# Block-sparse attention and a maxout feed-forward on one core: one PE visit per unit for scores and for values, single PSUM banks, queries of 256

## The chip, the core and the metric

The kernel runs on one core of one Trainium2 chip. Five engines work side by side there: PE (matrix products, which read on-chip memory and write PSUM, eight banks of 128 x 512 fp32), DVE (vector work), ACT (activation functions, copies), POOL (vector work that cannot reach PSUM, and gathers) and SP (which issues most DMAs here). The metric is the time of one launch in device microseconds, as a median of runs. Lower is better.

## What is computed

For 4 batches and 8 heads, with 768 positions of width 64, attention runs over blocks of 32 positions. A query block sees its own block and its two neighbours, the first and the last block, and three blocks drawn for it; the first and the last query block see everything. A maxout feed-forward follows.

```python
scores = scale * np.matmul(q, k.transpose(0, 1, 3, 2))
mask = np.abs(blk_i - blk_j) <= window
mask = mask | (blk_i == 0) | (blk_j == 0) | (blk_i == n_blocks - 1) | (blk_j == n_blocks - 1)
...
scores = np.where(mask, scores, -1000000000.0)
attn = np.exp(scores - np.max(scores, axis=-1, keepdims=True))
attn = attn / (np.sum(attn, axis=-1, keepdims=True) + 1e-09)
...
h = np.maximum(np.maximum(x @ w1, x @ w2), x @ w3)     # x: 3072 x 512, h: 3072 x 768
return (h @ w_out).astype(np.float32)
```

The four weight matrices come as 64-bit floats (3.1 MB each), the rest as fp32.

## The kernel before, in words

**Precision.** Every product is made of three fp16 passes: each operand is split into a high part and a low remainder (`PASSES`: high x high, high x low, low x high). Before the split a tensor is scaled by a power of two that comes from its sum of squares (`scale_of`, L317).

**Units.** A batch has 12 units. Eleven are *sparse*: two neighbouring query blocks with all eight heads. One (`"G"`) is *global*: the first and the last block, which see all 768 keys. Before, the global unit comes first in a batch. Four units make a *tile* of 256 rows of `x`, so there are 12 tiles.

**A sparse unit** is worked in two items of four heads. `gather` (L586) copies a query block's key blocks into `kg` (DVE, POOL and ACT each one of the drawn blocks, DVE the window) and fetches the value rows from a copy in DRAM (`vscr`) by an indirect DMA on POOL's queue. `sparse_item` (L663) then has: 24 matmuls of scores into a pair of banks (L677); on DVE the row maximum (L656) and from it the bias of the exponential (L658); two exponentials on ACT (L686); `probs` (L619), which splits the probabilities into high (ACT, L635) and low (POOL, L636) and turns them with a DMA transpose (L639), or, in the first four units, turns them on PE (L628); and 48 matmuls of values into `av_ps` (L701). `finish_unit` (L752) divides by the sums, turns the result on PE (L768) and splits it into `xg`. A global unit has four items of one head pair member each, with 12 matmuls of 384 columns of scores (L720) and 36 of values (L742).

**The feed-forward** (`feed_forward`, L779) of a tile makes 18 groups of 12 matmuls (L795, moving operand 256 wide), of which three at a time are reduced by a maximum (ACT L799, DVE L802), splits the result (ACT L805, POOL L806), and makes 2 x 3 groups of 6 matmuls of 512 columns (L819); ACT scales them (L825) and SP stores them.

**PSUM.** Two pairs of banks for scores (`s_pss`), one bank for values, two for the feed-forward in turn, one for everything that is turned or summed (`tp_one`); early on, one score pair may serve for turning too.

**Preparation.** K is loaded, squared for its sum (ACT, L462), turned on PE (L492) and split; V likewise without turning, and written to `vscr` (L524). Q comes in 24 tiles of 128 queries (L534 on), each with its square pass (L543), its scale (L319 to L324, L550, L551), a turn (L559) and a split. The weights are decoded from 64-bit patterns by hand (`decode_w`, L348): 24 loads land in four buffers (parts of `kt` and `xg`), POOL casts one part (L371), DVE joins it (L375) into a buffer in `ht`, ACT squares it (L386), and ACT and DVE split it (L398, L406).

**What sets the order.** Nothing is ordered at run time: every step is entered with `plan.add(engine, cost, ...)`, and `Plan.order` (L76) simulates the engines with these costs, always taking the ready step with the smallest `pri`. On PE it prefers feed-forward after feed-forward unless an attention step has waited over 3 us or more than two wait. The result is one fixed list of instructions for each engine; on the chip each engine runs its list in that order and waits on semaphores.

## Time and profile before

| what | us |
|---|---|
| median of 3 runs | 695.38 (691.42 to 697.71) |
| span of the profiled execution | 687.5 |
| median above that span | 7.9 |
| PE busy | 591.3 |
| DVE busy | 411.8 |
| ACT busy | 392.1 |
| POOL busy | 316.8 |

The profile gives the profiled execution's span, from its first to its last instruction, and no wall time of that same execution; the third row of the table is the distance of the median run to it. In the forty slices of the page the granted PE clock is between 0.5 and 0.6 in most of the first tenth to quarter, and 0.9 or more after it:

```profile
PE   2586468359999979999999789989999789999997
PEclk9756559559999989999999999999999999999999
```

Each digit is a slice of 17.2 us, in tenths. A line such as `L795 PE MATMUL f_ps<-xg,w_hl 128*128 128x256 f16 x2592 | 308.4, 278 | ...` names the source line, the engine, the operation, what it writes and reads, shape and count, then busy time, the mean duration in ns, and the idle time ahead of it. Matmuls overlap, so their mean duration (278 ns) is not what one of them costs; the distance between starts is.

### The profile page before, as it was taken

To read this page: it belongs to the slowest core of one execution; us is meant where nothing else is said; L and a number is where in the kernel's file an instruction comes from. 1 tells how busy PE (TensorE), PEld (TensorE's weight loads), DVE (VectorE), ACT (ScalarE), POOL (GpSimd) and SP (SyncE) were. 2 spreads that over 40 slices of the span, in tenths; PEclk is the share of its full clock that TensorE was granted. 3 is DMA by queue.
4 is the path that set the end of the run, shared out by engine and by line. 5 is a ranking of instruction groups with operands and counts; after the bars stand their busy time and mean duration, and the time that the engine had idled before them with its cause. 6 is when DMAs were issued, how large, how long until landed. Compare 5 with 4: busy or idle time off the path is not lost.

```text
span 687.5 us, 25107 instructions
## 1 busy us (share of the span) xinstructions
PE 591.3 (86%) x10576; PEld 442.2 (64%) x10576; DVE 411.8 (60%) x1022; ACT 392.1 (57%) x830; POOL 316.8 (46%) x414
## 2 busy tenths in 40 slices
PE   2586468359999979999999789989999789999997
PEld 2354347236885856875876666866776675778684
DVE  1678779983666876498555664676547675422110
ACT  4646667667636766776547656855558556312121
POOL 1354356463534665364554563446455756511110
PEclk9756559559999989999999999999999999999999
DMA  9684788779967799987997889996987979830000
GB/s 212 187 249 131 233 217 202 159 151 221 222 121 169 92 200 211 199 198 165 169 169 138 148 177 174 195 234 132 188 126 148 176 144 174 175 61 25 17 17 32
DMA packets 197044, 109.28 MB, mean 159 GB/s; under 512 B 161073, under 2 KB 182594, under 8 KB 196930
## 3 DMA queue, kind: packets, MB, share of 16 engines
q1 hardware_dynamic: 187074, 72.51, 57.1%
q0 software_dynamic: 9856, 35.15, 20.5%
q8 instruction: 83, 1.36, 0.9%
q14 instruction: 31, 0.25, 0.1%
HBM read 68.72 MB, written 12.70 MB: 118 GB/s over the span
## 4 chain that ended last, share of the span: by engine, by line
PE 70%; DVE 13%; issue 9%; ACT 2%; DMA 2%; POOL 1%; SPq 1%; DVEq 0%; POOLq 0%; ACTq 0%
PE f_ps L795 37%; PE f_ps L819 13%; PE av_ps L701 5%; PE s_ps L677 4%; PE s_ps L720 2%; DVE nm L656 2%; PE tp_ps L559 2%; PE tp_ps L492 1%; DVE nm L658 1%; PE tp_ps L768 1%; PE tp_ps L332 1%; DVE w_hl L406 1%; DVE vhl L520 1%; DVE kg L602 1%; PE av_ps L742 1%
## 5 line engine op out<-in xcount | busy, mean ns | idle before, releaser
L795 PE MATMUL f_ps<-xg,w_hl 128*128 128x256 f16 x2592 | 308.4, 278 | 15.7 <-issue 7.3
L795 PEld LDWEIGHTS <-w_hl 128*128 128x128 f16 x2592 | 254.6, 100 | 58.4 <-issue 23.5
L636 POOL TENSOR_TENSOR phl<-pr,phl 128x512 f16<-128x512 f32 (+1 forms) x106 | 119.1, 1130 | 81.1 <-ACT phl L635 51.8
L802 DVE SCALAR_TENSOR_TENSOR hf<-f_ps,hf 128x256 f32<-128x256 f32 x144 | 60.7, 421 | 114.6 <-PE f_ps L795 103.3
L806 POOL TENSOR_TENSOR ht<-hf,ht 128x256 f16<-128x256 f32 x72 | 50.4, 701 | 147.2 <-ACT ht L805 147.0
L686 ACT ACTIVATE pr<-s_ps,nm,qsm 128x256 f32<-128x256 f32 x176 | 92.2, 564 | 40.7 <-DVE nm L658 27.9
L608 POOL DMA_INDIRECT vg<-vscr,rows_of x88 | 83.6, 950 | 53.4 <-PE av_ps L701 37.2
L819 PE MATMUL f_ps<-wo_hl,ht 128*128 128x512 f16 x432 | 98.7, 380 | 0.0
L656 DVE TENSOR_REDUCE nm<-s_ps 128x2 f32<-128x512 f32 x88 | 60.2, 684 | 24.9 <-PE s_ps L677 18.5
L805 ACT CAST ht<-hf 128x256 f16<-128x256 f32 x72 | 28.9, 403 | 79.0 <-DVE hf L802 78.9
L819 PEld LDWEIGHTS <-ht 128*128 128x128 f16 x432 | 40.8, 98 | 46.9 <-issue 3.1
L635 ACT CAST phl<-pr 128x512 f16<-128x512 f32 (+1 forms) x106 | 61.7, 592 | 5.7 <-DMA pts<-phl 5.3
L595 POOL COPY kg<-kt 128x256 f16 x88 | 37.9, 450 | 53.8 <-PE s_ps L677 41.1
L701 PE MATMUL av_ps<-vg,pts 128*32 128x65 f16 (+1 forms) x4224 | 50.3, 200 | 13.2 <-issue 7.4
L701 PEld LDWEIGHTS <-pts 128*32 128x32 f16 x4224 | 41.5, 98 | 29.0 <-issue 20.9
L677 PE MATMUL s_ps<-kg,qt 64*32 64x256 f16 x2112 | 48.5, 294 | 10.8 <-ACT pr L686 4.4
L658 DVE TENSOR_SCALAR nm<-nm,qsm 128x2 f32<-128x2 f32 (+1 forms) x104 | 46.5, 448 | 2.2
L799 ACT ACTIVATE hf<-f_ps 128x256 f32<-128x256 f32 x72 | 27.5, 382 | 30.8 <-PE f_ps L795 30.3
L595 ACT COPY kg<-kt 128x256 f16 x88 | 32.7, 404 | 16.7 <-PE s_ps L677 13.2
L677 PEld LDWEIGHTS <-qt 64*32 64x32 f16 x2112 | 24.3, 95 | 22.7 <-issue 13.3
L825 ACT ACTIVATE ob<-f_ps,vsm 128x512 f32<-128x512 f32 x24 | 16.5, 686 | 26.9 <-PE f_ps L819 26.8
L595 DVE COPY kg<-kt 128x256 f16 x88 | 30.6, 381 | 1.5 <-issue 1.3
(138 smaller groups left out, 661.2 us busy)
## 6 DMA issues: line engine op xcount, KB each, us to landing
kt<-in_moe_w_dram SPq DMA_DIRECT2D x14, 511.0 KB, 4.1
vscr<-vhl SPq DMA_DIRECT2D x12, 520.0 KB, 4.5
stage<-in_k_dram SPq DMA_DIRECT2D x24, 256.0 KB, 5.6
stage<-in_v_dram SPq DMA_DIRECT2D x12, 512.0 KB, 8.0
qn<-in_q_dram SPq DMA_DIRECT2D x20, 256.0 KB, 5.0
out_dram<-ob SPq DMA_DIRECT2D x20, 256.0 KB, 2.1
vg<-vscr SPq DMA_DIRECT2D x16, 130.0 KB, 3.8
kt<-in_moe_w_out_dram SPq DMA_DIRECT2D x4, 511.8 KB, 4.6
```

Of the source, the lines that this page charges most:

```text
L595: (A.copy if t == 2 else eng.tensor_copy)(out=dst, in_=src)
L608: plan.add("POOL", 1.02, lambda c=c: L.indirect_dma_start(out=vgj[: 6 * HB, c].rearrange("p e h x -> p (e h x)"), out_offset=None, in_=vsc ...
L635: plan.add("ACT", 0.05 + 0.565 * n / 512, lambda: A.copy(out=hl[:, :n], in_=prt[:, :n]), r=[("pr", it % NPR)], w=[hk], pri=pri)
L636: plan.add("POOL", 1.2 * n / 512, lambda: L.tensor_tensor(out=hl[:, n : 2 * n], in0=prt[:, :n], in1=hl[:, :n], op=ALU.subtract), r=[("pr", ...
L656: plan.add("DVE", 0.7, lambda: V.tensor_reduce(out=n[:, 0:2], in_=both()[:, :, :256], axis=AX.X, op=ALU.max), w=[ks], pri=pri, drop=job)
L658: plan.add("DVE", 0.23, lambda: V.tensor_scalar(out=n[:, 2 : 2 + w], in0=n[:, :w], scalar1=sm[:, 5:6], scalar2=LN_TOP, op0=ALU.mult, op1=A ...
L677: T.matmul(out=s_ps[r * BS : (r + 1) * BS, hd * 512 : hd * 512 + 256], lhsT=q_t[hp, tq, 2 * i + u, q0 + c * BS : q0 + (c + 1) * BS], rhs=k ...
L686: plan.add("ACT", 0.56, lambda hd=hd: A.activation(out=prt[:, hd * 256 : hd * 256 + 256], in_=s_of(job)[:, hd * 512 : hd * 512 + 256], fun ...
L701: T.matmul(out=av_ps[r * BS : (r + 1) * BS, 2 * i + hd, :w], lhsT=pv[:, tp, hd, e, r * BS : (r + 1) * BS], rhs=vgj[:, c, e, h, (D + 2) * t ...
L795: T.matmul(out=pf, lhsT=w_hl[f][:, j, g, wp], rhs=x[:, g, xp, :], start=g == 0 and n == 0, stop=g == G - 1 and n == 2)
L802: plan.add("DVE", 0.42, lambda h=h, pf=pf: V.scalar_tensor_tensor(out=h, in0=pf, scalar=2.0 ** -14, in1=h, op0=ALU.mult, op1=ALU.max), r=[ ...
L819: T.matmul(out=f2_ps, lhsT=hts[:, f, hp, t * P : (t + 1) * P], rhs=wo_hl[f // 3][:, f % 3, wp], start=f == 0 and n == 0, stop=f == NF - 1 ...
```

## The change

Nearly every function is touched. What it does:

1. **One visit for a unit.** `sparse_item` becomes `sparse_unit`: all 48 matmuls of a unit's scores are one step, head pair members in two single banks, and all 96 of its values one step. Probabilities are still made in two halves. The global unit has four score steps of 12 matmuls with both members of a head pair in one group, and two value steps of 72.
2. **Banks singly.** All eight banks are `psb[0..7]`; a step takes one (or two single ones) of any that is free, up to a limit by kind: scores 4, values 2, turns and sums 2, feed-forward 3, early turns 6.
3. **Queries of 256.** 12 Q tiles of 256 queries in place of 24 of 128; the rows of a tile are laid out in even and odd positions, so `xg` is read with runs of 32 elements.
4. **Sparse units first** in batch 0; in later batches the global unit leads its tile. The first 8 units (4 before) turn their probabilities on PE.
5. **Squares on PE** for batch 0's K, V and first Q tile and for all weights: the upper 16 bits of the fp32 words, read as bf16, are multiplied with themselves in 128 x 128 blocks, and DVE sums the diagonal. Later batches keep ACT's square passes.
6. **Weights decoded in place**, and into twelve landing places; POOL or ACT may cast.
7. The bias of the exponential goes from DVE to ACT, with one operation for a unit. The table of gathered rows is made on DVE from one load of the sampled blocks. The first K and Q are loaded with longer runs and turned by plain fp32 matmuls with the identity.
8. **The planner** gets new costs, a model of the clock, of a port that DVE and POOL share and of DMA, and ranks each step by the due time of the feed-forward group that needs it, with written-out offsets for each kind of step (`OFFS`).

The core of the diff:

```diff
-    s_pss = [ps.tile([P, 1024], F32, name=f"s_ps{i}") for i in range(2)]
-    av_ps = ps.tile([P, 4, 65], F32, name="av_ps")
-    f_ps = [ps.tile([P, DM], F32, name=f"f_ps{i}") for i in range(2)]
-    tp_one = ps.tile([P, 512], F32, name="tp_ps")
+    psb = [ps.tile([P, 512], F32, name=f"ps{i}") for i in range(8)]
...
+    LIMIT = dict(s=4, a=2, t=2, f=3, k=6)
...
+    def squares_on_pe(parts, pri):
...
+                hi = top(view)
+                for y in range(0, n, P):
+                    T.matmul(out=bank(j)[:, :P], lhsT=hi[:, y : y + P], rhs=hi[:, y : y + P],
+                             start=x == 0 and y == 0, stop=x == len(parts) - 1 and y == n - P)
...
+        plan.add("DVE", 0.25, lambda: V.scalar_tensor_tensor(
+            out=junk[:, :P], in0=bank(j)[:, :P], scalar=1.0, in1=ident, op0=ALU.mult, op1=ALU.mult, accum_out=ssq[c]),
...
-            plan.add("DVE", 0.69, lambda st=st, k=k, y=y: V.scalar_tensor_tensor(
-                out=mi[:, k], in0=st.bitcast(I32).rearrange("p (x w) -> p x w", w=2)[:, :, 0], scalar=13, in1=y,
+            plan.add("DVE", 0.6, lambda st=st, y=y: V.scalar_tensor_tensor(
+                out=st.bitcast(I32)[:, :512], in0=st.bitcast(I32).rearrange("p (x w) -> p x w", w=2)[:, :, 0], scalar=13, in1=y,
...
+            for hd in range(2):
+                c0 = ((2 * g + hd) * 2 + e) * D
+                T.matmul(out=tv(y)[hd * D : hd * D + D], lhsT=st[:, c0 : c0 + D], rhs=ident, start=True, stop=True)
...
-        plan.add("DVE", 0.23, lambda: V.tensor_scalar(
-            out=n[:, 2 : 2 + w], in0=n[:, :w], scalar1=sm[:, 5:6], scalar2=LN_TOP, op0=ALU.mult, op1=ALU.add),
+        plan.add("ACT", 0.2, lambda: A.activation(
+            out=nb[:, 4:8], in_=nb[:, 0:4], func=AF.Identity, bias=ln_top, scale=sm[:, 5:6]),
...
+            for i in range(2):
+                for n, (tq, tk) in enumerate(PASSES):
+                    for r in range(4):
+                        u, c = r // 2, r % 2
+                        for hd in range(2):
+                            hp = slice(hd * 64, hd * 64 + 64)
+                            T.matmul(
+                                out=bank(j, hd)[r * BS : (r + 1) * BS, i * 256 : i * 256 + 256],
...
+        plan.add("PE", 0.70, scores, r=QK(F) + KG(jg), w=["s_turn"], pri=pri, mode="s", take=j, lat=0.95, cold=0.7)
...
+        plan.add("PE", 0.78, values, r=keys + VG(jg), w=["a_turn", ("unit", U)], pri=pri, mode="a", take=av, lat=1.0, cold=0.4)
...
-                            T.matmul(out=pf, lhsT=w_hl[f][:, j, g, wp], rhs=x[:, g, xp, :],
+                            T.matmul(out=bank(fj)[:, :256], lhsT=w_hl[f][:, j, g, wp], rhs=x[:, :, xp, :, g].rearrange("p n e x -> p e n x"),
...
-    order = ["G", NU - 1] + list(range(NU - 1))
+        for n in (2, 0, 1) if b else (0, 2, 1):
+            ms = [4 * n + x for x in range(4)]
+            ms = [m if m < 11 else "G" for m in ms]
+            if n == 2 and b:
+                ms = ["G"] + ms[:3]
```

More of the change, by code (lines that the diff above doesn't have):

```diff
@@ L134, in order @@
+            for job, k in op.drop:
+                job["left"][k] -= 1
+                job["end"][k] = max(job["end"][k], done + self.HOP)
+                if not job["left"][k]:
+                    banks[job["banks"][k]] = slots[job["kind"]][job["slots"][k]] = job["end"][k]
             for s in succ[i]:
[L135 to L136 removed]
+                ready[s] = max(ready[s], done + self.HOP)
@@ L137, in order @@
                 left[s] -= 1
                 if not left[s]:
-                    cands[ops[s].eng].add(s)
-        self.times = out
-        return [ops[i].emit for _, i in sorted(out)]
+                    for e in ops[s].forms:
+                        cands[e].add(s)
+        self.times, self.by = out, by
+        self.end = max(free.values())
+        return [ops[i].forms[by[i]][3] for _, i in sorted(out)]
 @with_exitstack
@@ new lines, in registers @@
+    def registers(t, name, first, pri):
+        blocks = slice(first, min(first + TB, NB - 1))
+        n = blocks.stop - blocks.start
+        def load():
+            _, values = nc.values_load_multi_w_load_instructions(
+                samp[0:1, blocks, t, 0], engines=[(ET.DVE, ET.Pool, ET.Activation)[t]], min_val=0, max_val=NB - 1)
+            for x, value in enumerate(values):
+                regs[t, first + x] = value
+        plan.add(name, 0.35 + 0.25 * n, load, r=["samp"], w=[("regs", t, first + x) for x in range(n)], pri=pri)
@@ L883, in tile_block_sparse_attention_maxout_ffn @@
+    plan.rank(KN["start"], KN["tile"], KN["stretch"])
+    emits = plan.order(KN["hold"], KN["att"], KN["queue"])
     with tc.manual_schedule():
```

1106 lines of the change are left out of this document (618 added, 488 removed).

## The prediction, made before the changed kernel ran

> **What bounds the kernel now.** I read the page first (busy times, the forty slices, the chain), then the windows view cut where the work changes, then PE's groups and waits in the longest stretch.
>
> ```profile
> span 687.5 us, 25107 instructions
> PE 591.3 (86%) x10576; PEld 442.2 (64%) x10576; DVE 411.8 (60%) x1022; ACT 392.1 (57%) x830; POOL 316.8 (46%) x414
> PE 70%; DVE 13%; issue 9%; ACT 2%; DMA 2%; POOL 1%; SPq 1%; DVEq 0%; POOLq 0%; ACTq 0%
> ```
> ```profile
> 0.00:97.00 97.00, 53.20 (x822) 36.41 (x823) 65.77 (x158) 58.94 (x111) 39.48 (x74) 0.67 0.73 201
> 97.00:174.00 77.00, 56.65 (x1045) 40.42 (x1047) 56.12 (x134) 52.82 (x108) 39.48 (x45) 0.75 0.88 189
> 174.00:620.00 446.00, 417.86 (x8219) 315.93 (x8214) 279.01 (x705) 267.41 (x584) 229.81 (x284) 0.98 0.89 166
> 620.00:687.50 67.50, 63.55 (x508) 49.47 (x506) 10.93 (x27) 12.90 (x29) 8.02 (x12) 1.00 0.06 21
> ```
> In the window rows the columns after the length are the busy time of PE, its weight loads, DVE, ACT and POOL, then the granted clock, the DMA share and GB/s. Four stages show. Until 97 us no feed-forward matmul can run: PE is busy 53.2 of 97 at a clock of 0.67 and DVE, at 65.8, is the busiest. From 97 to 174 only the first of the twelve feed-forward tiles is done, with PE idle for 77.0 - 56.65 = 20.35 us. From 174 to 620 PE is busy 417.9 of 446 (94%) at clock 0.98: it is the bound there, and 28.1 us is idle. At the end two tiles run alone:
>
> ```profile
> 620.85 23.58 PE f_ps L795 x216
> 644.43 7.77 PE f_ps L819 x36
> 652.20 23.58 PE f_ps L795 x216
> 675.78 7.78 PE f_ps L819 x36
> ```
> A tile is thus 23.58 + 7.77 = 31.35 us of matmuls at full clock (109 and 216 ns each), twelve are 376 us. The change leaves these matmuls as they are, so 376 us is the part that no schedule shortens; what can go is the time before and around them.
>
> The profiled execution's span is 687.5; the runs' median of 695.38 lies 7.9 us above it (the fastest run 3.9). I work with the span and add 7.9 at the end. A measurement of this kernel can tell about 1% from no change.
>
> **Stage 1, until the first feed-forward matmul (97 us).** Removed from the path: the six small loads of sampled blocks and POOL's long row of small operations for the row table (now one load and DVE work), the ACT square passes of batch 0 and of the weights (now 128x128 bf16 products on PE and a diagonal sum on DVE), the global unit as first unit (sparse units come first), and the reuse of four landing buffers for weights. Added: K and Q of the first tile are turned by plain fp32 matmuls, and units 4 to 7 also have their probabilities turned on PE. PE is idle for 97 - 53.2 = 43.8 us here, which covers the added PE work; without that cover it would cost its own time: 8 turns of 8 matmuls, from 8 times the 1.09 us of the old turn (9 us, bound 0 net) to 64 times the longest row for a cold fp32 matmul here, 0.415 us (27 us, so 18 more).
>
> ```profile
> 14.19 1.09 PE L492 MATMUL s_ps<-ident,stage 128*128 128x128 f32 x4
> ```
> ```profile
> L492 PE MATMUL s_ps<-ident,stage 128*128 128x128 f32 x16 | 4.0, 415 | 3.6 <-DVE qt L564 2.8 <-DVE vsm L319 0.8
> ```
> The Trainium skill (Perfetto Trace Analysis, Transposes) says to use the transpose and not a standard matmul for a transpose, which speaks against these turns. The row above shows only the transpose; if the page's loss were all exposed, the sum would be up to 18 us higher.
>
> The start is then set by DVE, whose list hardly shrinks. It has no data for about 10 us; 65.8 us of work at 98% occupancy gives 10 + 67 = 77 us. So I take -20 us, with bounds 0 (DVE just as loose as now) and -27 (four units at 70 us).
>
> **Stage 2, the first tile beside the weights (77 us).** Before, its second product could start only when the last weights were split:
>
> ```profile
> L375 DVE SCALAR_TENSOR_TENSOR ht<-xg,ob x6: 680/683/746, 51.2 to 140.7; 128x512 int32<-128x512 int32 x6
> L398 ACT ACTIVATE wo_hl<-ht,w_t x6: 707/710/721, 147.0 to 151.4; 128x512 f16<-128x512 f32 x6
> L819 PE MATMUL f_ps<-wo_hl,ht x432: 376/380/391, 164.4 to 683.2; 128*128 128x512 f16 x144
> ```
> The columns after the name are min/median/max in ns and the first and last start. Decoding ran from buffer to buffer until 141 us, over these loads and ten like them:
>
> ```profile
> kt<-in_moe_w_dram SPq DMA_DIRECT2D x14, 511.0 KB, 4.1
> ```
> With the decoded form written into the landing place, all 24 loads (12.3 MB) have a place early; at the 201 GB/s of stage 1 they alone need 61 us, so they can have landed by 80 to 100 us beside K, Q and V. PE's 20.35 us of idle goes, and most of the half-rate excess of this tile:
>
> ```profile
> L795 PE MATMUL f_ps<-xg,w_hl 128*128 128x256 f16 x216 | 29.5, 303 | 4.6 <-ACT hf L799 4.6
> ```
> 29.5 against 23.58 is 5.9 us. Together -26.3 at most, 0 at least; I take -24, since the first few us will still be at half clock. Four more turned units put 56 + 24 = 80 instead of 48 transposes of probabilities on PE: 32 more at 0.2 us (between 0.27 us for two warm ones, the two starts below, and 0.41 us for a cold one) is +6 us, bounds +4 and +13.
>
> ```profile
> L628 PE MATMUL tp_ps<-ident,pr 128*128 128x128 f32 x17 | 4.6, 411 | 2.5 <-ACT pr L730 2.1 <-DVE pts L631 0.4
> 326.18 0.44 PE L768 MATMUL tp_ps<-ident,xr 128*128 128x128 f32 x2
> 326.45 4.09 PE L795 MATMUL f_ps<-xg,w_hl 128*128 128x256 f16 x36
> ```
>
> **Stage 3, PE-bound (446 us).** One visit in place of two is cheap to price from neighbours: the start of the next visit minus the start of this one.
>
> ```profile
> 309.29 0.56 PE L701 MATMUL av_ps<-vg,pts 128*32 128x65 f16 x48
> 309.77 0.52 PE L677 MATMUL s_ps<-kg,qt 64*32 64x256 f16 x24
> 310.23 0.56 PE L701 MATMUL av_ps<-vg,pts 128*32 128x65 f16 x48
> ```
> ```profile
> 304.17 0.98 PE L701 MATMUL av_ps<-vg,pts 128*32 128x65 f16 x96
> 305.09 0.33 PE L492 MATMUL tp_ps<-ident,stage 128*128 128x128 f32 x1
> ```
> ```profile
> 382.12 0.85 PE L677 MATMUL s_ps<-kg,qt 64*32 64x256 f16 x48
> 382.89 0.59 PE L701 MATMUL av_ps<-vg,pts 128*32 128x65 f16 x52
> ```
> Half a unit's values take 0.48, a whole one 0.92; half a unit's scores 0.46, a whole one 0.77. So a unit gains at most 0.04 + 0.15 us, and if all of the 1584/48 = 33 sparse units here came in halves, 6 us; 22 units' scores and some values do, so -4 (0 to -6). The headline of the change is worth little by itself.
>
> The global scores gain more: they now run both heads of a pair in one group, four tiles of the array at a time, where 12 matmuls used two:
>
> ```profile
> 209.19 1.16 PE L720 MATMUL s_ps<-kt,qt 64*64 64x384 f16 x12
> 210.29 0.44 PE L768 MATMUL tp_ps<-ident,xr 128*128 128x128 f32 x2
> ```
> 1.10 us each, and 144/12 = 12 of them here; at half, -6.6 (bounds 0 and -6.6; that head pairs do run together the sparse scores show, 24 matmuls of 256 columns in 0.46 us). The sums of squares have a bf16 instead of an fp32 product and half as many Q tiles: the three groups below (10.5 us) come down to about 16 visits of some 0.3 us, -5 (-3 to -8).
>
> ```profile
> L332 PE MATMUL tp_ps<-qsm,ones 128*128 128x1 f32 x36 | 6.6, 252 | 0.7 <-DVE xg L773 0.7
> L332 PE MATMUL tp_ps<-vsm,ones 128*128 128x1 f32 x18 | 2.4, 247 | 0.0
> L332 PE MATMUL tp_ps<-ksm,ones 128*128 128x1 f32 x12 | 1.5, 237 | 0.0
> ```
> The 28.1 us of idle is what freer banks should cut: any job may take any of eight banks, feed-forward groups have three instead of two, scores four single ones, and the values their own two.
>
> ```profile
> L795 PE MATMUL f_ps<-xg,w_hl 128*128 128x256 f16 x1944 | 231.4, 277 | 11.0 <-issue 7.3 <-DVE hf L802 3.7
> L701 PE MATMUL av_ps<-vg,pts 128*32 128x65 f16 (+1 forms) x3504 | 38.9, 195 | 7.6 <-issue 7.4 <-DVE xr L761 0.2
> L658 DVE TENSOR_SCALAR nm<-nm,qsm x104: 203/228/3021, 32.5 to 592.2; 128x2 f32<-128x2 f32 x88, 128x1 f32<-128x1 f32 x16
> ACT pr L686 <- DVE nm L658: 27.9, 22, 5.6
> ```
> The bias of the exponential also leaves DVE, where an operation of 228 ns sometimes lasted 3.0 us and ACT waited 27.9 us for it, for one ACT operation per unit. I take -18 of the 28 (0 to -25). Strided reading of the feed-forward's moving operand (runs of 32 elements) I cost at nothing: the sparse scores already read runs of 16 at full rate. Off PE: DVE loses the 104 bias operations and half of the Q scalings; ACT, POOL and SP stay below two thirds busy.
>
> **Stage 4.** The two lone tiles are not shortened by the change; PE does the same work sooner or later.
>
> **The sum.** -20 - 24 + 6 - 4 - 6.6 - 5 - 18 = -71.6; 687.5 - 71.6 = 615.9; + 7.9 = **624 us**. All best bounds together (-27 - 26 + 4 - 6 - 6.6 - 8 - 25 = -95) give 601, all worst (+18 + 13 - 3) 723.
>
> **Rivals.**
> *Start not shortened* (0.13): DVE, not the landing places, paces the weights: 24 decodes and 24 splits stay on it. For: it is the busiest engine of both first stages. Against: decode waited for its inputs and buffers. Then stage 1 stays and stage 2 gives 10 of its 24: 624 + 20 + 14 = 658 us. The Trainium skill (SBUF — State Buffer, Who interferes with whom) says that a DVE operation with two SBUF inputs and a GpSimd operation reading SBUF exclude each other for their whole length; the decode and POOL's cast remain such a pair, and the 3.0 us operation above agrees, so I keep this rival above a tenth.
>
> *DMA is the bound of stage 3* (0.11):
>
> ```profile
> q1 hardware_dynamic: 133024, 44.68, 62.7%
> q0 software_dynamic: 7840, 27.96, 25.3%
> DMA to landing us min/median/max: 2.8/5.9/10.4
> ```
> In stage 3 the queues' packets fill 62.7 + 25.3% of sixteen engines, and transposes and gathers per unit stay the same. If 0.89 is all there is, stage 3 keeps its length and only stages 1 and 2 gain: 624 + 4 + 6.6 + 5 + 18 = 658 us. Against: PE's waits there name no DMA.
>
> *Values hold the queue* (0.05, the slower side): PE's order is fixed, and a unit's values now start only when both its transposes have landed (2.8 to 10.4 us). Each us of lateness stalls PE with the feed-forward behind it. From 78 us over the forecast it is slower by 1%: 44 sparse units by 1.8 us each, giving 702 us. Against: 7.6 us of idle before the values in all of stage 3.
>
> *All gains near their best* (0.15): about 601 us.
>
> *Forecast* 0.56.
>
> **How the numbers follow.** Low 596 (just under the best case, with a tenth below), high 662 (both 658 rivals in, the slow one and the bad bounds out). Faster by over 1% holds in the forecast, both 658 cases and the best case: 0.95, less 0.03 for a forecast that fails in several steps at once; within 1% 0.03, slower 0.05.
>
> **What would show it.** First feed-forward matmul near 77 us and its second product below 115; PE idle from there to the last unit near 10 us; global scores 12 matmuls in 0.55 us; a tile every 43 to 45 us; no operation on DVE between maximum and exponential. Wrong if the first tile starts after 90 us, if PE's idle after it exceeds 30 us, or if values wait for transposes.

## The result and the profile after

The changed kernel takes 645.04 us (median of 4 runs, 643.53 to 648.83) where the kernel before takes 696.55 (691.42 to 701.44, 4 runs): a ratio of 0.932, 95% interval 0.925 to 0.938 (the two medians alone give 0.926). The prediction said 624, range 596 to 662. Runs that lie over 1.5% above the fastest run of the same kernel count as slow and are not held against fast ones; where that leaves a variant below with one run, the text gives that run. The variants ran at other times and on other chips, so below each ratio is to the kernel before as it ran beside the variant.

The profiled execution took 648.83 us with a span of 647.0, so 1.8 us lie around the span. First the page after, the lines that answer to those of before:

```profile
span 647.0 us, 25220 instructions
PE 575.5 (89%) x10784; PEld 437.9 (68%) x10784; DVE 351.6 (54%) x935; ACT 385.6 (60%) x842; POOL 286.4 (44%) x369
q1 hardware_dynamic: 172304, 70.46, 58.0%
q8 instruction: 84, 1.38, 0.9%
```

PE is still the busiest engine and is busy for 15.8 us less; DVE's busy time fell by 60. The span fell by 40.5. (The page's chain of after breaks off after a third of the span, so it is not used.) The windows view, cut at the same events as before (first feed-forward matmul, end of the first tile, last attention matmul):

```profile
0.00:76.20 76.20, 43.55 (x861) 32.52 (x862) 48.15 (x149) 37.33 (x74) 25.61 (x42) 0.75 0.89 243
76.20:148.30 72.10, 63.76 (x1158) 48.26 (x1156) 62.22 (x161) 56.85 (x120) 21.07 (x30) 0.93 0.66 163
148.30:590.60 442.30, 415.77 (x8362) 317.20 (x8360) 232.16 (x605) 280.75 (x627) 232.98 (x288) 0.98 0.91 171
590.60:647.00 56.40, 52.44 (x411) 39.89 (x408) 9.08 (x22) 10.62 (x24) 6.69 (x10) 0.99 0.05 20
```

Subtract the second number of a row from the first: PE idles 8.3 us in stage 2 (20.35 before) and 26.5 us in stage 3 (28.1 before). Stage 1 is 20.8 us shorter, stage 2 4.9 us, and from the first tile's end to the end of the span the time falls from 513.5 to 498.7, by 14.8.

So that work and idle time add up, I give each matmul the time from its start to the start of the next one, less what PE was idle in between, and sum that by kind over the whole program:

| PE time, us | before | after | change |
|---|---|---|---|
| feed-forward | 392.9 | 389.5 | -3.4 |
| scores of sparse units | 44.0 | 44.1 | +0.1 |
| values of sparse units | 46.4 | 43.5 | -2.9 |
| global scores | 20.7 | 10.3 | -10.4 |
| global values | 12.7 | 12.7 | 0 |
| sums and squares | 16.6 | 16.2 | -0.4 |
| turns of K, Q, probabilities, units | 57.7 | 58.9 | +1.2 |
| idle between matmuls | 83.3 | 60.8 | -22.5 |
| before the first matmul | 8.9 | 6.8 | -2.2 |

That is the 40.5 us (the 4.4 us from the last matmul's start to the end are the same in both and left out). The step that gives the change its name, one visit for a unit's scores and one for its values, is worth 2.8 of it. More than half is idle time, nearly all of it in stages 1 and 2.

The waits of PE in stage 3 (engine, line, what it waited for; us in all, times, longest) show what the 26.5 us are:

```profile
PE ps L814 <- issue: 5.6, 10, 1.6
PE ps L814 <- ACT kg L740: 3.8, 1, 3.8
PE ps L977 <- POOL phl L785: 3.2, 1, 3.2
PE ps L901 <- issue: 2.8, 5, 1.2
PE ps L846 <- issue: 2.4, 4, 1.4
PE ps L954 <- DVE xg L934: 2.2, 1, 2.2
PE ps L977 <- issue: 2.1, 2, 1.3
```

No row is a wait for a bank, and half of the time (14.0 us) has "issue" behind it: PE waited for nothing that the profile shows. In the timeline such a stop stands in the middle of a visit, after 17 of 48 matmuls that all have their data:

```profile
519.49 0.50 PE L814 MATMUL ps<-kg,qt 64*32 64x256 f16 x17
521.57 0.63 PE L814 MATMUL ps<-kg,qt 64*32 64x256 f16 x31 [1.58 <-issue]
```

Count PE's instructions from the program's start, from 0, with weight loads and the waits on semaphores, and most of the larger stops stand at one place: number 193 or 194 of a block of 256. After: at 190.5, 240.6, 249.0, 293.9, 521.6, 527.1 and 544.3 us, 9.2 us together. The one at 249.0 is the 3.2 us that the view puts down to POOL (L785); it stands in the middle of a run of equal matmuls, at number 194, and goes with the others in an experiment below, so I count it here. Before, ten of them, 17.5 us: all of the 7.3 and 7.4 us of "issue" that the prediction quoted, and 2.8 us within scores. The q8 line above says where blocks of 256 come from: 84 packets for 21,568 PE instructions, 256.8 for each. A block of PE's instructions arrives by DMA, and each of these stops ended 1.2 to 1.6 us after the end of a q8 packet, before and after the change. Why the place is 193 and not 0 the profile doesn't show. Most blocks come in time, since 256 feed-forward instructions take some 14 us; a unit's scores and values are 288 instructions in 1.7 us.

### The profile page after: what moved, and what is told of

Same layout as the page of the kernel before. It is cut to its first block, busy times and chain, and to the rows that moved or that the text cites. A ratio compares the mean times of both kernels' runs of the same rounds, so it can differ in the third digit from the quotient of the medians.

```text
span 647.0 us, 25220 instructions
## 1 busy us (share of the span) xinstructions
PE 575.5 (89%) x10784; PEld 437.9 (68%) x10784; DVE 351.6 (54%) x935; ACT 385.6 (60%) x842; POOL 286.4 (44%) x369
## 5 line engine op out<-in xcount | busy, mean ns | idle before, releaser
L954 PE MATMUL ps<-xg,w_hl 128*128 128x256 f16 x1728 | 203.0, 273 | 5.0 <-DVE xg L934 2.2
L954 PEld LDWEIGHTS <-w_hl 128*128 128x128 f16 x1728 | 166.3, 98 | 34.7 <-issue 9.7
L785 POOL TENSOR_TENSOR phl<-pr,phl 128x512 f16<-128x512 f32 (+1 forms) x98 | 108.5, 1116 | 60.5 <-ACT phl L784 34.7
L962 DVE SCALAR_TENSOR_TENSOR hf<-ps,hf 128x256 f32<-128x256 f32 x144 | 60.7, 421 | 125.4 <-PE ps L954 108.0
L796 ACT ACTIVATE pr<-ps,nm,qsm 128x256 f32<-128x256 f32 (+1 forms) x208 | 113.4, 589 | 10.7 <-POOL phl L785 9.7
L977 PE MATMUL ps<-wo_hl,ht 128*128 128x512 f16 x432 | 105.5, 389 | 7.2 <-POOL phl L785 3.2
L954 PE MATMUL ps<-xg,w_end 128*128 128x256 f16 x864 | 103.0, 276 | 2.0 <-DVE w_end L532 1.2
L954 PEld LDWEIGHTS <-w_end 128*128 128x128 f16 x864 | 83.6, 99 | 15.4 <-issue 2.9
L822 DVE TENSOR_REDUCE nm<-ps 128x2 f32<-128x512 f32 x88 | 56.8, 683 | 49.3 <-PE ps L814 33.3
L977 PEld LDWEIGHTS <-ht 128*128 128x128 f16 x432 | 40.9, 100 | 54.0 <-issue 11.8
L965 ACT CAST ht<-hf 128x256 f16<-128x256 f32 x72 | 29.5, 409 | 61.3 <-DVE hf L962 60.8
L740 ACT COPY kg<-kt 128x256 f16 x88 | 32.9, 415 | 46.3 <-PE ps L814 24.1
L814 PE MATMUL ps<-kg,qt 64*32 64x256 f16 x2112 | 46.8, 283 | 11.4 <-issue 7.5
L846 PE MATMUL ps<-vg,pts 128*32 128x65 f16 (+1 forms) x4224 | 46.4, 198 | 7.8 <-issue 6.7
```

The source lines that it names most:

```text
L740: (A.copy if t == 2 else eng.tensor_copy)(out=dst, in_=src)
L785: plan.add("POOL", 0.03 + 1.07 * n / 512, lambda: L.tensor_tensor(out=hl[:, n : 2 * n], in0=prt[:, :n], in1=hl[:, :n], op=ALU.subtract), r ...
L796: plan.add("ACT", 0.46 if n == 256 else 0.57, lambda j=j, b=b, c0=c0, col=col, x=x: A.activation(out=pr[it % NPR][:, x * n : x * n + n], i ...
L814: T.matmul(out=bank(j, hd)[r * BS : (r + 1) * BS, i * 256 : i * 256 + 256], lhsT=q_t[hp, tq, 2 * i + u, q0 + c * BS : q0 + (c + 1) * BS], ...
L822: plan.add("DVE", 0.6, lambda hd=hd: V.tensor_reduce(out=nb[:, 2 * hd : 2 * hd + 2], in_=bank(j, hd).rearrange("p (i x) -> p i x", i=2), a ...
L846: T.matmul(out=a_ps[r * BS : (r + 1) * BS, 2 * i + hd, :w], lhsT=pv[:, tp, hd, e, r * BS : (r + 1) * BS], rhs=vgj[:, c, e, h, (D + 2) * tv ...
```

## The experiments

### Four edits, with the planner free to make another order

Theory at this point: the gain is what the change does (start, pairing, sums), and the idle time of stage 3 is not a matter of banks. Rival: much of the gain is the written-out order (`OFFS`).

**No offsets.**

```diff
-            op.pri = t + OFFS[t >= start + tile].get(op.name, 0.0)
+            op.pri = t
```


> The written-out offsets are dropped; every step, cost and due time stays, so the same instructions stand in another order. Structure (the prediction's view: visits, banks, pairing and the start carry the gain): 645 to 665 us, first feed-forward matmul within 5 us of 76, PE idle from 148 us to the last unit below 45. Rival, order (the offsets carry most of the 51 us): 690 us or more, with PE idle of that stage above 60.

Measured: 673.11 us (four runs, 662.88 to 682.84), ratio 0.975 (0.964 to 0.986). The profiled run is the fastest, 662.88 with a span of 661.1 (0.954 of the median of the kernel before beside it); the other three took 673 us and more. In its profile the first feed-forward matmul is at 81.8, the first tile done at 155.0, the idle of stage 3 30.5 us. That run and its idle lie in the first theory's bands, the first matmul just beyond its; the median lies between the bands of the two theories. By that one run the offsets are worth some 18 us (662.88 - 645.04), over a third of it before the first tile's end; by the median it is more.

**Heads apart.**

```diff
-                    for n, (tq, tk) in enumerate(PASSES):
-                        for u in range(2):
-                            for hd in range(2):
+                    for hd in range(2):
+                        for n, (tq, tk) in enumerate(PASSES):
+                            for u in range(2):
```


> The global scores' twelve matmuls are issued one head of the pair after the other, with nothing else changed. Pairing (the prediction's view): a visit goes from 0.61 back to about 1.1 us, sixteen visits are 7.7 us, twelve of them in the PE-bound stage: 650 to 653 us. Rival, the saving came from the single banks: a visit stays near 0.61, 645 us.

Measured: 645.52 us, ratio 0.931; a visit takes 0.627 us (0.614 interleaved). The pairing as I put it, by interleaving, fell. The starts showed why: the second head's first matmul starts 20 ns after the first head's first, though four matmuls stand between them in the list. That asked for the barrier below.

**Two visits.**

```diff
-        plan.add("PE", 0.70, scores, r=QK(F) + KG(jg), w=["s_turn"], pri=pri, mode="s", take=j, lat=0.95, cold=0.7)
+        for i in range(2):
+            def half_scores(i=i):
+                scores(i)
+            plan.add("PE", 0.35, half_scores, r=QK(F) + KG(jg), w=["s_turn", ("sc", U)], pri=pri, mode="s", take=None if i else j, lat=0.60, cold=0.35)
...
+        for i in range(2):
+            def half_values(i=i):
+                values(i)
+            plan.add("PE", 0.39, half_values, r=keys[i] + VG(jg), w=["a_turn", ("unit", U)], pri=pri, mode="a", take=None if i else av, lat=0.61, cold=0.2)
```


> Scores and values of a sparse unit are again two steps each (24 and 48 matmuls), so another step may stand between them and the first half of the values waits for its own half of the probabilities alone. By the prices of visits (0.04 + 0.15 us for a unit) 44 units lose at most 8 us: 645 to 653. Rival, instruction blocks: dense visits are what outruns the fetch of PE's instructions, so halves with feed-forward between them lose fewer of the 12.5 us of stops in the middle of visits and of the 18 us of waits for data: 635 to 643. Rival, more changes of kind on PE: above 655.

Measured: 678.88 us, ratio 0.977 (0.967 to 0.986), 34 us over the changed kernel. A half took 0.454 and 0.489 us as in the kernel before, so the prices were right, and yet the loss is far above them. By its size it is the third case; the run without offsets on either side, below, speaks against that.

**Squares on ACT.** The squares of batch 0 and of the weights as ACT passes, as before the change:

```diff
-        sq, drop = squares_on_pe(parts, pri)
+        ws = w_sq[g % 2]
+        for x, (view, n, keys) in enumerate(parts):
+            plan.add("ACT", 0.65, lambda x=x, view=view: A.activation(out=junk[:, :512], in_=view, func=AF.Square, accum_out=ws[:, x : x + 1]),
...
+        sq, drop = total([ws[:, x : x + 1] for x in range(3)], [("wsq", g % 2, x) for x in range(3)], pri)
```


> The squares of batch 0's K, V and first Q tile and of the weights go back to ACT: 7 passes of 1.15 us and 24 of 0.65 us, 23.7 us, on an engine that is busy 94 of the first 148 us. Off the path: first feed-forward matmul at 76 to 80, first tile done within 4 us of 148, 645 to 650 us. Rival, the squares set the start: first feed-forward matmul at 84 or later, first tile done 8 us later or more, 653 to 665 us.

Measured: 679.62 us, ratio 0.981 (0.971 to 0.991), first feed-forward matmul at 85.9 us, as the rival had it. But the loss isn't where the edit is: the first tile is done at 141.1 us, 7 us *earlier* than in the changed kernel, and the loss lies behind it (535.5 us from there to the end, 498.7 in the changed kernel), where no square was changed:

```profile
141.10:624.00 482.90, 438.81 (x8534) 330.97 (x8533) 236.48 (x617) 285.91 (x637) 234.37 (x291) 0.95 0.84 157
```

Held against the third row of the changed kernel above, PE's idle is 44.1 us (26.5 there) and its granted clock 0.95 (0.98 there). So both edits carried a second one with them: the planner made another order, for which the offsets were not made. From here on I change what a step emits and keep its place.

### Order held, or the offsets gone on both sides

**Squares on ACT, order kept.** The planner still sees PE squares; ACT passes are emitted in their places.

```diff
-                hi = top(view)
-                for y in range(0, n, P):
-                    T.matmul(out=bank(j)[:, :P], lhsT=hi[:, y : y + P], rhs=hi[:, y : y + P],
-                             start=x == 0 and y == 0, stop=x == len(parts) - 1 and y == n - P)
+                for y in range(0, n, 512):
+                    z = x * (n // 512) + y // 512
+                    A.activation(out=bank(j), in_=view[:, y : y + 512], func=AF.Square, accum_out=w_sq[c][:, z : z + 1])
```


> The squares of batch 0's K, V and first Q tile and of the weights go back to ACT at the places where PE had them, with the order of everything else kept (in the run before the planner was free to make another order). ACT gets 38 passes of 512 elements at some 0.65 us, 25 us, in the first 150 us; PE loses 13.7 us of square matmuls and DVE most of its diagonal sums. Order (the loss of the run before came from the new order): 642 to 655 us, stage from the first tile's end to the end 499 us as before. Rival, ACT (the squares on ACT themselves cost the start): first tile done 15 us later or more, 660 to 685 us.

Measured: 653.15 us, ratio 0.937 (0.930 to 0.943), against 0.932 (0.925 to 0.938) of the changed kernel. First feed-forward matmul 80.5, first tile done 153.6, 5.3 us later; stage 3 439.9 us with 24.1 idle. So the order cost 26 of the 35 us, and squares on PE are worth 3 us by the ratios, 5 by the first tile's end and 8 by the medians; the two intervals overlap. The granted clock up to the first feed-forward matmul was 0.65 here and 0.75 in the changed kernel, so whether ACT's time or PE's lower clock makes the 5 us these runs don't tell apart.

**Two visits, no offsets on either side.** The edits of "two visits" and of "no offsets" together.

> Two visits for scores and for values as in that run, but without the written-out offsets, to be held against the run without offsets alone (span 661.1 us, 673 us median), so that neither order has offsets made for it. Order (the offsets fit only the steps they were made for, and the visits are worth the few us of their prices): within 8 us of that run, 660 to 680. Rival, visits (single halves cost the 34 us themselves): 690 us or more.

Measured: 667.34 us where the kernel before took 688.49 beside it; without offsets alone it was 673.11 beside 694.83. Both are 0.969 of the kernel before by the medians, and by their fastest runs, the only ones to be compared (655.42 and 662.88), 0.952 and 0.954. So the visits as such make no difference that can be measured, on one run each and with an order of its own in each.

**Heads with a barrier.** Heads apart, and between them one matmul that needs the whole array:

```diff
+                        if hd == 1:
+                            T.matmul(out=bank(js[e])[:, 511:512], lhsT=ones, rhs=ones[:, 0:1], start=True, stop=True)
```


> Global scores with one head after the other, as in the run with heads apart, and between the two heads one matmul of a single column over the whole array, which no matmul of the second head can pass. If the two heads of a pair run at the same time on four parts of the array even where they are not interleaved (0.627 us with heads apart), the visit is now 1.05 to 1.2 us, sixteen visits cost 7 to 9 us more, 650 to 655 us. Rival, two parts of the array suffice and the saving against the kernel before came from elsewhere: 0.65 to 0.7 us, 645 us.

Measured: 648.12 us, ratio 0.943 (0.937 to 0.949), against 0.932: about 1%, in line with the 7 to 9 us, though the intervals touch. The visit takes 1.32 us (98.96 - 97.64 below), 0.7 more than without the barrier, over the band that I gave.

```profile
97.64 0.68 PE L871 MATMUL ps<-kt,qt 64*64 64x384 f16 x6
98.25 0.18 PE L867 MATMUL ps<-ones 128*128 128x1 bf16 x1
98.35 0.68 PE L871 MATMUL ps<-kt,qt 64*64 64x384 f16 x6
98.96 0.96 PE L846 MATMUL ps<-vg,pts 128*32 128x65 f16 x96
```

Six matmuls of one head alone take 0.61 us, and twelve of both, without the barrier, take 0.61 to 0.63. So the two heads do run at once on four parts of the array, and all that it needs is both in one step: as the starts of the run with heads apart showed, PE starts a later matmul for a free part ahead of earlier ones in the list.

### What stops PE in the middle of a visit

Theory: late instruction blocks. Rivals: data or semaphores at these visits; DMA load that makes blocks late.

**Half a block more at the start.**

```diff
+            if emit.__name__ == "pool":
+                for _ in range(64):
+                    T.matmul(out=psb[7][:, 0:1], lhsT=ones, rhs=ones[:, 0:1], start=True, stop=True)
```


> Right at the start, where PE waits for its first data anyway, 64 one-column matmuls are added (128 PE instructions with their weight loads), and every engine's order is kept. Instruction blocks: PE's stops in the middle of a visit stand at one place of the blocks of 256 instructions that the instruction queue brings (194 of 256), so they keep that place and move to other visits by half a block: the stops at 190.5, 249.0, 521.6, 527.1 and 544.3 us go, others come, and the span changes by up to 6 us either way. Rival, semaphores or data: the stops stay at the same visits, half a block off in the count, and the span is 643 to 647 us.

Measured: 646.93 us, ratio 0.928 (0.923 to 0.934). In the shifted kernel the values of one unit are cut where they ran through before:

```profile
378.69 0.97 PE L846 MATMUL ps<-vg,pts 128*32 128x65 f16 x94
384.59 0.24 PE L846 MATMUL ps<-vg,pts 128*32 128x65 f16 x2 [4.93 <-issue]
```

The stops at the visits of 190.5, 249.0, 521.6, 527.1 and 544.3 us are gone. New ones stand at 234.7 (2.2 us), 285.9 (1.8), 311.9 (0.6), 384.6 (4.9) and 426.7 (0.5): 10.0 us, each again at instruction 193 or 194 of a block. The waits for data stay with their visits, as the shifted kernel's waits show (compare the changed kernel's above):

```profile
PE ps L901 <- issue: 4.1, 5, 1.3
PE ps L814 <- ACT kg L740: 3.8, 1, 3.8
PE ps L954 <- DVE xg L934: 2.2, 1, 2.2
```

Instruction blocks it is, for those stops (the 3.2 us at 249.0 that the view gave to POOL went with them); five small ones within the global values (L901) stay and are something else.

**Half the transposes.**

```diff
-            out=ptt[:, : 2 * n].rearrange("p (n x) -> p n x", x=P),
-            in_=hl[:, : 2 * n].rearrange("p (n x) -> p n x", x=P), transpose=True),
+            out=ptt[:, :n].rearrange("p (n x) -> p n x", x=P),
+            in_=hl[:, :n].rearrange("p (n x) -> p n x", x=P), transpose=True),
```


> The DMA transposes move only the high half of the probabilities and leave the low halves as they were in the landing buffers (this part of the computation is left out); order and everything else stay. DMA load (busy queues make the instruction blocks and the gathered rows late): q1's packet time falls from 58% to below 45%, PE idle between the first tile's end and the last unit from 26.5 to below 16 us, 630 to 636 us. Rival, the lateness is that of the fetch itself and of the engines' order: idle stays within 22 to 30 us, 642 to 647 us.

Measured: 647.56 us, ratio 0.930 (0.924 to 0.936).

```profile
q1 hardware_dynamic: 125200, 58.40, 43.1%
```
```profile
147.80:590.60 442.80, 415.30 (x8362) 317.38 (x8361) 232.21 (x605) 280.52 (x627) 234.09 (x288) 0.98 0.71 144
```

The DMA share of stage 3 falls from 0.91 to 0.71, and PE idles 27.5 us as before. DMA load is out as a cause, and with it the prediction's rival that DMA bounds stage 3.

**Feed-forward groups moved ahead of the stops.** Feed-forward groups moved at seven places of PE's list, all else in place:

```diff
-    emits = plan.order(KN["hold"], KN["att"], KN["queue"])
+    plan.order(KN["hold"], KN["att"], KN["queue"])
+    emits = plan.moved([(2069, 3), (2769, 1), (2915, 3), (3790, 3), (8887, 1), (9014, 1), (9390, 1)])
```


> Nine feed-forward groups are issued ahead of the visit in which PE stopped (at 158.6, 190.5, 197 to 202, 249.0, 521.6, 527.1 and 544.3 us of the changed kernel's profile, 16 us of stops in all); every other engine's order and all banks are kept. If those stops are waits for something that comes at its own time (an instruction block, a copied key), 1.3 us of work in front of each takes up to its own length away: 634 to 641 us. Rival: the stops come again at the next dense visit, 643 to 648 us.

Measured: 646.82 us, ratio 0.928 (0.923 to 0.933): no gain. Its profile is of a run of 656.66 us, so I compare no single stops. At 249.0 us, by the order of PE's matmuls, no other work came ahead of the stop than before. Moving what stands beside a late block by hand did not pay here.

**Gathers by plain DMAs.** The five small stops that stayed put have something beside them. In the changed kernel, PE and POOL:

```profile
196.24 1.29 PE L901 MATMUL ps<-vhl,pts 128*64 128x65 f16 x52
196.69 0.94 POOL L753 DMA_INDIRECT vg<-vscr,rows_of  x1
197.93 0.91 POOL L753 DMA_INDIRECT vg<-vscr,rows_of  x1 [0.30 <-issue]
197.97 0.29 PE L901 MATMUL ps<-vhl,pts 128*64 128x65 f16 x5 [0.45 <-issue]
198.86 0.27 PE L901 MATMUL ps<-vhl,pts 128*64 128x64 f16 x4 [0.60 <-issue]
199.15 0.91 POOL L753 DMA_INDIRECT vg<-vscr,rows_of  x1 [0.30 <-issue]
199.58 0.29 PE L901 MATMUL ps<-vhl,pts 128*64 128x65 f16 x6 [0.45 <-issue]
200.37 0.91 POOL L753 DMA_INDIRECT vg<-vscr,rows_of  x1 [0.31 <-issue]
201.03 0.26 PE L901 MATMUL ps<-vhl,pts 128*64 128x65 f16 x5 [1.16 <-issue]
202.57 1.86 PE L977 MATMUL ps<-wo_hl,ht 128*128 128x512 f16 x4 [1.28 <-issue]
```

Four indirect DMAs are issued in a row, and through them PE advances by four to six matmuls at a time.

```diff
-            plan.add("POOL", 1.2, lambda c=c: L.indirect_dma_start(
-                out=vgj[: 6 * HB, c].rearrange("p e h x -> p (e h x)"), out_offset=None, in_=vscr[b],
-                in_offset=bass.IndirectOffsetOnAxis(ap=rows_of[:, i0 + c : i0 + c + 1], axis=0),
-            ), r=VSCR(b) + ["rows_of"], w=[("vg", j % 2, c)], pri=pri, land=2.2, move=1.65)
+            plan.add("POOL", 1.2, lambda c=c: Y.dma_start(
+                out=vgj[: 6 * HB, c].rearrange("p e h x -> p (e h x)"), in_=vscr[b][: 6 * HB, :]), r=VSCR(b) + ["rows_of"], w=[("vg", j % 2, c)], pri=pri, land=2.2, move=1.65)
```


> The value rows of a unit come by plain DMAs on SP's queue, 96 fixed rows of the same size, in place of POOL's indirect DMAs (the choice of the rows is left out; bytes, keys, order and places stay). Gathers (POOL's issue of them holds up other engines: four in a row stand beside PE's five small stops at 197 to 202 us, in the middle of one visit, and pairs of them beside the late instruction blocks at 249.0, 521.6 and 544.3): the small stops go, the late blocks get fewer, PE idle between the first tile's end and the last unit falls from 26.5 to 14 to 19 us, 633 to 640 us. Rival, the blocks are late by themselves: idle 23 to 29 us, 642 to 648 us.

Measured: 624.95 us, ratio 0.910 (0.905 to 0.916), 2.3% below the changed kernel (0.910 / 0.932), the largest gain of any single edit here.

```profile
0.00:70.60 70.60, 37.92 (x860) 29.45 (x861) 47.58 (x148) 37.13 (x73) 14.35 (x30) 0.83 0.96 259
70.60:138.60 68.00, 59.90 (x1158) 45.57 (x1157) 62.16 (x162) 56.77 (x119) 15.64 (x23) 1.00 0.69 176
138.60:564.30 425.70, 406.99 (x8362) 314.03 (x8361) 234.81 (x605) 280.28 (x627) 168.77 (x218) 0.99 0.92 178
```

Stage 3 is 16.6 us shorter with the same matmuls and nearly the same DMA share (0.92, 0.91 in the changed kernel): 7.8 us of idle and 8.8 of time that counted as work. The five small stops are gone, and with them every stop of stage 3 with "issue" behind it that does not stand at number 193 or 194 (7.9 us in the changed kernel). Of the 8.8 us, one part is pauses shorter than a matmul, which are not seen as idle. Another is the clock: in stage 3 of the changed kernel the granted clock falls to 0.5 four times for 3.4 us (from 158.2, 202.6, 250.4 and 462.0 us), each time within 1.5 us of the end of a stop of 1.3 to 3.8 us; here it does so twice. By the clock 3.4 us then hold 1.7 us of work, so two times fewer are some 3.4 us.

Stages 1 and 2 are 9.7 us shorter too. The clearest place is a visit of 48 scores in stage 1: beside four issues it takes 5.8 us in the changed kernel (from 39.9 us), and here 1.5 (from 39.8).

Adding up by how much each sparse visit exceeds its undisturbed length (0.785 us for scores, 0.93 for values; visits over by at least 0.25): beside an indirect DMA's issue 10.05 us in the changed kernel (1.6 of it the late block at 521.6, which stands in both sums) and 0 here, elsewhere 10.7 and 12.7. My theory's second half fell: late blocks do not become fewer (nine with 10.5 us, six of them at instructions where the changed kernel has one, against 9.2). So two causes stand side by side: blocks, and POOL's issue of gathers.

**Half the rows by POOL.** The whole computation, with the window rows by plain DMAs; to see whether it pays:

```diff
+                for p, n, r in {1: [(0, 1, zero), (1, 2, two)], NB - 2: [(0, 2, one), (2, 1, zero)]}.get(
+                        i, [(0, 3, slice((i - 1) * HB, (i + 2) * HB))]):
+                    Y.dma_start(out=vgj[p * HB : (p + n) * HB, c].rearrange("p e h x -> p (e h x)"), in_=vscr[b][r, :])
+                L.indirect_dma_start(
+                    out=vgj[3 * HB : 6 * HB, c].rearrange("p e h x -> p (e h x)"), out_offset=None, in_=vscr[b],
+                    in_offset=bass.IndirectOffsetOnAxis(ap=rows_of[: 3 * HB, i : i + 1], axis=0))
```


> The whole computation, with half as many rows gathered by POOL: the three window blocks of a query block lie side by side in memory and come by one plain DMA on SP's queue, and the indirect DMA brings only the 48 rows of the drawn blocks (96 before); every engine's order is kept. Rows (what holds PE up is the number of rows that POOL's issue has to describe): half of the gain of the run with plain gathers, 634 to 640 us, POOL's operation near 0.5 in place of 0.91 us, the excess of visits beside a gather's issue from 10 to about 5 us. Rival, each issue costs the same whatever its rows: 0.91 us as before, excess near 10, 642 to 648 us with SP's 88 DMAs more.

Measured: 674.41 us, ratio 0.973 (0.968 to 0.978): 30 us slower, outside both cases.

```profile
L759 POOL DMA_INDIRECT vg<-vscr,rows_of x88: 871/877/1133, 39.3 to 604.0; - x88
```
```profile
142.60:619.30 476.70, 432.36 (x8507) 326.67 (x8506) 236.95 (x618) 285.36 (x636) 234.09 (x290) 0.96 0.86 159
```

The issue takes 877 ns with 48 rows and 913 with 96, so POOL's time hangs on the number of issues and hardly on the rows, as the rival said; the loss neither case foresaw. PE idles 44.3 us in stage 3, and its granted clock is 0.96 there in place of 0.98. Visits beside an issue exceed by 24.4 us, and late blocks take 20.1 us, two of them 4.9 and 4.5 (at least 5.8 us stand in both sums). Why both are that much larger here is not settled; 96 DMAs more on SP are not enough by themselves, since the run with plain gathers had 88 on SP and gained.

## Why the prediction was right, and where it was wrong

The direction was right, and the time lies in the range, 21 us above the forecast. The sum said a span of 615.9; it is 647.0, 31.1 us more. The profiled execution has 1.8 us around its span where I had added 7.9, and is itself 3.8 us above the median: 31.1 - 6.1 - 3.8 = 21.2. Of the 31.1 us, stage 2 has 13.1 and what follows it 18.8; stage 1 was 0.8 better. Nearly all errors lie on one side, and the time is in the range because its high end was set to hold two rivals that did not come.

- **Stage 1 (-20 us): right.** First feed-forward matmul at 76.2, forecast 77. The reason holds in part: squares on PE were worth 5.3 us at the first tile's end, within the noise of the runs; what the landing places, the row table and the order of units give apart wasn't tried. PE idles 32.6 us here, so the 128 plain matmuls that turn the first K and Q (L572, 11.0 us) did not show as a loss.
- **Stage 2 (-24 and +6): the first failed step.** It shrank by 4.9 us, not by 18. "PE's 20.35 us of idle goes" was wrong on both counts. PE's idle fell by 12.0 us, to 8.3; the first tile's own matmuls, of which 5.9 us were to go, fell from 36.3 to 33.4; and what left stage 1 came here: PE work other than feed-forward rose from 20.1 to 30.4 us, 6.7 of it the global unit (4 visits of scores and 2 of values, in stage 1 before), 6.7 the 48 transposes of probabilities (near the +6, but by luck: the prediction had 32 more at 0.2 us, and 48 came at 0.14), 3.6 squares of weights, 3.5 turns of the next K. A move was booked as a gain in the stage it left and not as a cost in the stage where it lands. And "all 24 loads have a place early" failed: decoding in place keeps a place until its weights are split. SP waited for each of the second twelve loads, six of w1 to w3 and six of w_out:

```profile
L502 SPq EVENT_SEMAPHORE  x12: 17/22/28, 67.9 to 82.7; - x12
L505 SPq EVENT_SEMAPHORE  x12: 17/28/28, 84.9 to 107.7; - x12
L532 DVE SCALAR_TENSOR_TENSOR w_hl<-kt,w_s,w_hl x3: 743/743/748, 67.1 to 72.4; 128x512 f16<-128x512 f32 x3
L532 DVE SCALAR_TENSOR_TENSOR wo_hl<-kt,w_t,wo_hl x3: 743/743/744, 134.9 to 136.2; 128x512 f16<-128x512 f32 x3
L977 PE MATMUL ps<-wo_hl,ht x432: 376/379/634, 132.4 to 642.7; 128*128 128x512 f16 x144
```

 The first place comes free when its low part is split (67.1, for 0.74 us); the next load is issued at 68.0, the last one at 107.7, and the last split starts at 136.2. So the second product starts at 132.4, where I had asked for 115. PE itself waited only 1.4 and 0.4 us for these weights (before L977); it had other work by then, so the late weights left it little idle time.
- **Visits (-4): the right order of size.** -2.8 over the whole program, nothing within stage 3 (values 35.6 us before and after). The planner before already set halves side by side: its 73 halves of values stood in 51 visits.
- **Global scores (-6.6): right**, in stage 3 they fell from 12.4 to 7.4 us (12 visits by 1.10 - 0.61 would be 5.9); the four visits ahead of stage 3, in part at the lower clock, fell from 8.3 to 2.9. The mechanism is shown by the barrier.
- **Sums of squares (-5): right in kind.** 8.0 us before and 1.3 after in stages 3 and 4, -6.7.
- **Idle of stage 3 (-18): the second failed step.** It went from 28.1 to 26.5. The prediction had quoted the rows "issue 7.3" and "issue 7.4" and counted them for freer banks. They were instruction blocks, which no bank touches. Late blocks did fall, 17.5 to 9.2 us (why, no run here shows), but what isn't late blocks rose from 10.6 to 17.3. In the kernel before those 10.6 us were all waits for DVE; in the changed one the waits for other engines are 8.7 us, the longest 3.8 for ACT and 2.2 for DVE, and 7.9 us are "issue" pauses at other places of the block. The kernel before had no such pauses in stage 3, and they went with the gathers' issues. (Visits beside an issue exceeded by 5.6 us before, but 2.8 of that are late blocks.) The bias of the exponential behaves as I said, and gives nothing: ACT's wait for DVE's bias (27.9 us) is replaced by this one, off the path:

```profile
ACT pr L796 <- POOL phl L785: 9.7, 17, 1.3
```

 The Trainium skill (Runtime: NRT & Kernel Launch, Instruction fetch mechanics) says that an engine's instructions are refilled in blocks of 256 and that crossing a boundary is mostly hidden. The block size agrees with the 256.8 instructions for a packet here; "mostly hidden" does not hold for dense visits, which lost 17.5 us before and 9.2 after in stage 3.
- **Rivals.** The start was shortened, against the first. (The 3.0 us operation that the prediction took as a witness for it reads one tensor and a column of scalars; beside it on POOL, at 404.0 us, stood a gather's issue and then a split of probabilities, so it doesn't show the case of two tensors.) DMA bounds nothing in stage 3, as half the transposes showed. No wait of PE ahead of values names a DMA, so they do not hold the queue. The three marks that the prediction set: a tile each 45.0 us (494.8 us for eleven tiles, 46.4 before), at the edge of 43 to 45; idle of 26.5, neither near 10 nor over 30; values without waits for transposes.

Open stays how a gather's issue on POOL holds up PE, whether it is POOL's work or the transfers of its queue that do it, why the blocks came so late with the window rows on SP, and how much of stage 1 the landing places give.

## What to carry to other kernels

A kernel whose order is fitted by hand or by search can't be taken apart by edits that let the planner order anew: two such edits seemed to cost 34 and 35 us, and with the order held, or the offsets gone on both sides, the same edits cost nothing measurable and 3 to 8. Before a stall is credited to a cure, its kind must be known: a stop in the middle of a visit, with "issue" behind it, waited for neither bank nor data here; count the instructions up to it, and look at what POOL issues beside it. And when work is moved out of a stage, book it where it lands before that stage's idle time is counted as gain.

## What the runs showed of the hardware that I had not expected

- PE's instructions come in blocks of 256, a weight load and a matmul counting one each. Visits that run through 288 of them in 1.7 us outran the blocks: 17.5 us of stops before, 9.2 after, and with half a block more at the start every one of these stops in the changed kernel went and others came, at the same place of the block.
- While POOL issues an indirect DMA (0.91 us, whether for 96 rows or, at 0.88, for 48), a dense visit of small matmuls on PE pauses by some 0.3 to 0.6 us at a time, now and then over 1 us. Feed-forward matmuls beside such an issue kept their pace (median 109 ns from start to start with and without). Without these issues, with the choice of the rows left out, the kernel took 625 us.
- A head's six matmuls of 64 x 64 fill two of four parts of the array; the other head's six, later in the same list, ran beside them and cost next to no time (0.61 us for one head, 0.63 for both one after the other in the list, 0.61 interleaved).
- A stop costs more than its length where the clock falls with it: about the end of stops of 2.6, 3.9 and 3.9 us in stage 3 of the kernel before (252.7, 393.9 and 547.9 us) PE was granted half the clock for 3.4 or 6.8 us, and four times for 3.4 us in the changed kernel. Not every stop of over 2 us did it: one of 2.5 us before (454.5) and one of 2.6 us with plain gathers (500.5) did not.
